# The decision of the fallback flag on VectorE, moved behind the last residual addition

## The chip, the cores and the metric

One core of one Trainium2 chip runs the whole kernel. The metric is device time in microseconds (us) of one execution; the kernel before took 322.09 us as the median of three runs (321.22, 322.09 and 322.19). The five engines are TensorE (PE; its weight loads are listed as PEld), VectorE (DVE), ScalarE (ACT), GpSimd (POOL) and SyncE (SP, which issues most DMAs). A "q" behind an engine's name, as in SPq, stands for its sequencer: instructions such as a DMA issue, a wait on a semaphore, the reading of a register or a branch, which the busy times don't count.

## What is computed

Four layers with residual additions, A, B, A, B, on x of 2048 x 512 in bfloat16, 32 heads of 16:

```python
x = A_x
x = x + _A_ref(_layernorm(x, axis=-1), A_wqkv, A_w_phi, A_wo)
x = x + _B_ref(_layernorm(x, axis=-1), B_wqkv, B_wo)
x = x + _A_ref(_layernorm(x, axis=-1), A_wqkv, A_w_phi, A_wo)
x = x + _B_ref(_layernorm(x, axis=-1), B_wqkv, B_wo)
return x
```

A is linear attention with a learned softmax feature map, B is sliding attention over 8 positions with a dilation of 2. Both end in a projection by `wo`, and its result is added to x.

## The kernel before

The program has two paths. The fast one (class `_Fast`) works on four token blocks of 512 tokens, b = 0 to 3, each held as `x[b]` with four tiles of 128 x 512, t = 0 to 3. It leaves out the subtraction of maxima in its softmaxes, which is right as long as the numbers stay small. Beside the work it gathers what tells whether they did: two sums of squares (`okc`, columns 0 and 1) and the sums of the exponentials and of their reciprocals (`stE`, `stR`). At its end it works out a flag, `fl`: 0 if all bounds hold, 1 if not. Every engine reads the flag into a register, and branches on it: with 0 it jumps over the second path (`_general_path`, a slow and safe version of the whole computation, L2063), with 1 it runs through it. With these inputs the flag is 0, so the second path isn't executed.

The flag is made by four steps in `s_flag`:

- `counts` (L1385 to L1390, DVE) compares the sums with their limits, and writes `okb`, 128 x 4.
- `total` (L1394, PE) sums `okb` over the partitions with a matmul of ones into PSUM.
- `decide` (L1398 to L1402, DVE) makes three small operations, each on the result of the one before: `ok` from the PSUM, `tot` from `ok`, `fl` from `tot`.
- `read` (L1413, all five engines) loads `fl` into a register; the branch of L2063 stands behind it.

The last layer's end is made by `s_out`. For each tile t of a block, four matmuls on PE (L542) form the projection in PSUM, one addition on DVE (L555) adds it to `x[b]`, and SP stores the result to HBM (L566). The last block to be finished, whose x is called `x_85` in the program's rows, is one of those in the table `split`: its tiles are stored one by one, 128 KB each, where other blocks store two tiles at a time, 256 KB. Each such store waits for the addition of its tile.

Behind the branch stand a few instructions on each engine: waits for its own semaphores (on SP eight of them, for the DMAs in flight; L2063 and L2090), a DRAIN, and a barrier of all five engines (L2090). The span of the profile ends with that barrier.

The order of the work is written out by hand. Each step is put on a thread by `add(stage, engine, ...)`; `run` walks through the table `_ORDER`, whose words are thread numbers in base 36, and calls the next step of that thread each time. An engine executes its instructions in just that order. The words of the flag are `iw` (DVE's thread: its first occurrence runs `counts`, its second `decide`), `ix` (`total`) and `iy` (`read`).

Of the kernel before, what the change touches and what calls it, by code (L numbers as in the profile page):

```python
# [96 lines left out]
if fh ig gb if ig gg ig gl gs ge gs fg ig gk gb gp gt gr gr gr gt ga gf ih ih if ig if ig du gr if if gs ih du  # L97
ig dv gt ii gt dw fd ig ij ij ii ik gu gu ij du gt du ij dy ik ih gu fe gs dz il gv fi gv ii ij ij im ik il fj
fk fj dx in fl iq fj ir fj dx fo iq fm is ii gw gw ij gv il ij gx ik gw il io gv gv fn fm iw gz iq ip iq iu it
gy iv it h2 gw h0 gw h2 ix iw h3 h4 h5 h3 h1 h2 h6 h3 h2 h3 h5 h7 h5 h8 h5 iy  # L100
"""


# [1991 lines left out]
```

## Time and profile before

| | us |
|---|---|
| median of three runs | 322.09 (321.22 to 322.19) |
| the profiled execution | 321.0 |
| its span, from the first to the last instruction | 319.3 |
| PE busy | 307.5 (96% of the span) |
| DVE busy | 295.6 (93%) |
| ACT busy | 274.7 (86%) |
| POOL busy | 47.3 (15%) |

The profiled execution took 321.0 us, 1.7 us more than its span: that is what lies ahead of the first and behind the last recorded instruction. Times "at 311.27" count from the start of the span. The granted TensorE clock was 0.996 of full speed. DMA share is the mean busy share of the core's 16 DMA engines, so that one engine of the 16 that works alone shows as 0.06. Issue to landing is the time from a DMA's issue on SP to the end of the last of its pieces; a store of 128 partitions is cut into 16 pieces, one for each DMA engine. The DMA queue called hardware_dynamic carries the kernel's transfers, the queues called instruction carry program code to the engines.

### The profile page before, as it was taken

To read this page: it belongs to the slowest core of one execution; us is meant where nothing else is said; L and a number is where in the kernel's file an instruction comes from. 1 tells how busy PE (TensorE), PEld (TensorE's weight loads), DVE (VectorE), ACT (ScalarE), POOL (GpSimd) and SP (SyncE) were. 2 spreads that over 40 slices of the span, in tenths; PEclk is the share of its full clock that TensorE was granted. 3 is DMA by queue.
4 is the path that set the end of the run, shared out by engine and by line. 5 is a ranking of instruction groups with operands and counts; after the bars stand their busy time and mean duration, and the time that the engine had idled before them with its cause. 6 is when DMAs were issued, how large, how long until landed. Compare 5 with 4: busy or idle time off the path is not lost. (4 is left out here: it accounts for less than half of the span.)

```text
span 319.3 us, 8889 instructions
## 1 busy us (share of the span) xinstructions
PE 307.5 (96%) x3572; PEld 152.5 (48%) x3572; DVE 295.6 (93%) x458; ACT 274.7 (86%) x638; POOL 47.3 (15%) x64
## 2 busy tenths in 40 slices
PE   8999999899999999999999999879999999999992
PEld 4644456445454444444444455534444444445550
DVE  6999995998999999999999999599997999999993
ACT  4999999999898778999999999799999777698560
POOL 6000000000004121000000000041240744035000
PEclk9999999999999999999999999999999999999998
DMA  7977100015795979949994500014389865565743
GB/s 197 351 197 154 30 2 4 2 23 146 180 156 113 153 137 137 137 83 120 158 127 54 69 0 2 4 35 117 89 171 137 149 123 127 129 163 136 172 141 132
DMA packets 45789, 36.37 MB, mean 114 GB/s; under 512 B 30832, under 2 KB 41136, under 8 KB 45744
## 3 DMA queue, kind: packets, MB, share of 16 engines
q1 hardware_dynamic: 45216, 35.75, 55.7%
q8 instruction: 29, 0.48, 0.7%
q14 instruction: 16, 0.13, 0.2%
q10 hardware_dynamic: 528, 0.02, 0.1%
HBM read 11.13 MB, written 3.25 MB: 45 GB/s over the span
## 5 line engine op out<-in xcount | busy, mean ns | idle before, releaser
L950 PE MATMUL PS<-xnT,WB 128*128 128x512 bf16 x336 | 76.8, 380 | 0.1
L1042 DVE TENSOR_TENSOR prod<-QT,K 128x4096 bf16<-128x4096 bf16 x28 | 63.4, 2287 | 0.5 <-POOL K L976 0.5
L1104 DVE TENSOR_TENSOR pav<-PT,Vg 128x4096 bf16<-128x4096 bf16 (+1 forms) x29 | 63.0, 2216 | 0.2
L950 PEld LDWEIGHTS <-WB 128*128 128x128 bf16 x336 | 37.4, 114 | 36.3 <-issue 3.3
L728 ACT ACTIVATE Eq<-PS 128x512 bf16<-128x512 f32 x64 | 36.3, 618 | 0.0
L621 ACT ACTIVATE Ek<-PS 128x512 bf16<-128x512 f32 x64 | 35.1, 623 | 0.2 <-PE PS L615 0.2
L542 PEld LDWEIGHTS <-oT 128*128 128x128 bf16 x240 | 22.3, 98 | 27.0 <-issue 1.3
L720 PE MATMUL PS<-xnT,WA 128*128 128x512 bf16 x128 | 32.0, 380 | 0.5 <-DVE s L812 0.3
L562 ACT ACTIVATE sqd<-x 128x512 bf16<-128x512 bf16 x48 | 30.0, 632 | 2.2 <-DVE x L555 2.0
L627 PE MATMUL PS<-WA,xnT 128*128 128x512 bf16 x128 | 31.6, 379 | 0.0
L555 DVE SCALAR_TENSOR_TENSOR x<-PS,x 128x512 bf16<-128x512 f32 x47 | 30.8, 685 | 0.3 <-PE PS L542 0.3
L615 PE MATMUL PS<-WA,xnT 128*128 128x512 bf16 x128 | 31.0, 379 | 0.0
L204 ACT CAST oT<-PS 128x512 bf16<-128x512 f32 (+1 forms) x50 | 26.8, 599 | 3.8 <-PE PS L1111 2.1
L542 PE MATMUL PS<-WoA,oT 128*128 128x512 bf16 x128 | 29.8, 380 | 0.0
L542 PE MATMUL PS<-WoB,oT 128*128 128x512 bf16 x112 | 27.4, 380 | 0.0
L204 ACT CAST K<-PS 128x512 bf16<-128x512 f32 x30 | 17.3, 594 | 3.1 <-PE PS L950 1.9
L615 PEld LDWEIGHTS <-xnT 128*128 128x128 bf16 x128 | 12.3, 98 | 15.1 <-issue 0.9
L627 PEld LDWEIGHTS <-xnT 128*128 128x128 bf16 x128 | 12.2, 98 | 14.5 <-issue 0.4
L673 DVE TENSOR_TENSOR Ek<-Ek,rk 128x4096 bf16<-128x4096 bf16 (+1 forms) x10 | 18.6, 1861 | 0.4 <-ACT rk L668 0.4
L465 DVE TENSOR_SCALAR xn<-x,rstd,nmr 128x512 bf16<-128x512 bf16 x48 | 18.2, 426 | 0.6
L720 PEld LDWEIGHTS <-WA 128*128 128x128 bf16 x128 | 11.6, 98 | 14.6 <-issue 1.7
L204 ACT CAST V<-PS 128x512 bf16<-128x512 f32 x26 | 15.2, 596 | 2.6 <-PE PS L950 2.6
(164 smaller groups left out, 501.6 us busy)
## 6 DMA issues: line engine op xcount, KB each, us to landing
Vg<-V SPq DMA_DIRECT2D x112, 131.5 KB, 4.3
Prho<-rd SPq DMA_DIRECT2D x8, 512.0 KB, 6.0
x<-in_A_x_dram SPq DMA_DIRECT2D x3, 512.0 KB, 6.7
WB<-in_B_wqkv_dram SPq DMA_DIRECT2D x3, 512.0 KB, 9.2
out_dram<-x SPq DMA_DIRECT2D x6, 256.0 KB, 2.2
wraw<-in_A_wqkv_dram SPq DMA_DIRECT2D x4, 256.0 KB, 4.4
vd<-Vs SPq DMA_DIRECT2D x2, 272.0 KB, 3.5
x<-in_A_x_dram SPq DMA_DIRECT2D x4, 128.0 KB, 4.6
```

What stands on the lines that cost most here:

```text
L204: self.nc.scalar.copy(out=out, in_=in_)
L542: nc.tensor.matmul(y[:], lhsT=lh(t, c), rhs=Wo()[:, c, :], start=(c == 0), stop=(c == NB - 1 and not onpe))
L555: nc.vector.scalar_tensor_tensor(out=xb[:, t, :], in0=T[t][:], scalar=1.0, in1=xb[:, t, :], op0=ALU.mult, op1=ALU.add, **kw)
L562: nc.scalar.activation(out=sqd[:], in_=xb[:, t, :], func=ACT.Square, accum_out=T["ss"][:, t:t + 1])
L615: nc.tensor.matmul(pk[:], lhsT=xnT[:, t, k, :], rhs=self.WA[:, k, D:2 * D], start=(k == 0), stop=(k == NB - 1))
L621: nc.scalar.activation(out=T["E"][:, t, s, :], in_=T["k", t][:], func=ACT.Exp, scale=1.0 - 2.0 * s)
L627: nc.tensor.matmul(pv[:], lhsT=xnT[:, t, k, :], rhs=self.WA[:, k, 2 * D:3 * D], start=(k == 0), stop=(k == NB - 1))
L720: nc.tensor.matmul(pq[:], lhsT=self.WA[:, k, hb * P:(hb + 1) * P], rhs=xnT[:, :, k, :], start=(k == 0), stop=(k == NB - 1))
L728: nc.scalar.activation(out=self.Eq[L, b][s][:, :, hb, :], in_=T[hb][:].rearrange("p (t i) -> p t i", t=4), func=ACT.Exp, scale=1.0 - 2.0 * s)
L950: nc.tensor.matmul(pp[:], lhsT=self.WB[:, k, i * D + c:(i + 1) * D:NB], rhs=xnT[:, :, k, :], start=(k == 0), stop=(k == NB - 1))
L1042: nc.vector.tensor_tensor(out=pr[:], in0=QT[:, c:c + 1, :].to_broadcast([P, NW, TB]), in1=win, op=ALU.mult)
L1104: nc.vector.tensor_tensor(out=pv, in0=PT[:, :, lo:lo + n].unsqueeze(1).to_broadcast([P, NB, 2, n]), in1=vw, op=ALU.mult)
```

## The change

One word of `_ORDER` moves: the second `iw`, which runs `decide`, goes from behind `ix` to a place behind the last additions.

```diff
-gy iv it h2 gw h0 gw h2 ix iw h3 h4 h5 h3 h1 h2 h6 h3 h2 h3 h5 h7 h5 h8 h5 iy
+gy iv it h2 gw h0 gw h2 ix h3 h4 h5 h3 h1 h2 h6 h3 h2 h3 h5 h7 h5 h8 iw h5 iy
```

On DVE the difference is this piece at the end of the fast path (names with a number are the program's buffers: `x_85` is the last block's x, `x_86` that of the block before it; `PS` is the PSUM):

```order
 L1390 TENSOR_TENSOR okb<-okc,sgn 128x4
 L555 SCALAR_TENSOR_TENSOR x_86<-PS,x_86 128x512 x2
+L555 SCALAR_TENSOR_TENSOR x_85<-PS,x_85 128x512 x4
 L1398 TENSOR_TENSOR ok<-PS,thr 128x4
 L1400 TENSOR_REDUCE tot<-ok 128x1
 L1402 TENSOR_SCALAR fl<-tot 128x1
-L555 SCALAR_TENSOR_TENSOR x_85<-PS,x_85 128x512 x4
 L1413 TENSOR_LOAD fl
 L2063 COMPARE_AND_BRANCH
```

The three operations of `decide` stood ahead of the four additions of the last block, and now stand behind them. Everything else on DVE keeps its order.

On SP, at the same place, nothing moves; these rows are the same before and after, each with the engines whose semaphores it waits for (DMAHW are those of earlier DMAs):

```order
L566 DMA out_dram<-x_85 128x512 [waits DMAHW0_49,DVE_49]
L566 DMA out_dram<-x_85 128x512 [waits DMAHW1_49,DVE_49]
L566 DMA out_dram<-x_85 128x512 [waits DMAHW2_49,DVE_49]
L566 DMA out_dram<-x_85 128x512 [waits DMAHW3_49,DVE_49]
L1413 TENSOR_LOAD fl [waits DVE_49]
L2063 COMPARE_AND_BRANCH
```

SP reads the flag behind its last store in both kernels. PE, ACT and POOL have the same rows in the same order too; each reads the flag as its last instruction ahead of the branch, and that reading waits for the moved `fl`.

## The prediction

> **What bounds the kernel now.** The page's busy table comes first, then its chain of work that ended last:
>
> ```profile
> PE 307.5 (96%) x3572; PEld 152.5 (48%) x3572; DVE 295.6 (93%) x458; ACT 274.7 (86%) x638; POOL 47.3 (15%) x64
> DVE x L555 0%
> ```
>
> PE and DVE are nearly full, but the change touches only the last 8 us. The chain ends on DVE's residual addition (L555) and says no more. The timeline of DVE and PE from 311.2 shows where that addition stands (start, duration, and so on):
>
> ```profile
> 311.27 0.16 DVE L1398 TENSOR_TENSOR ok<-PS,thr 128x4 f32<-128x4 f32 x1 [0.20 <-PE PS L1394]
> ...
> 311.66 0.15 DVE L1402 TENSOR_SCALAR fl<-tot 128x1 int32<-128x1 f32 x1
> 311.73 2.47 DVE L555 SCALAR_TENSOR_TENSOR x<-PS,x 128x512 bf16<-128x512 f32 x4
> 311.07 2.32 PE L542 MATMUL PS<-WoB,oT 128*128 128x512 bf16 x10
> ```
>
> DVE ends at 311.73 + 2.47 = 314.20, and the span at 319.3. So 5.1 us lie behind the last arithmetic, and what fills them is found on the sequencers. The reading of the flag (duration min/median/max in ns, then first and last start):
>
> ```profile
> L1413 ACTq TENSOR_LOAD <-fl x1: 714/714/714, 311.8 to 311.8; - x1
> L1413 PEldq TENSOR_LOAD <-fl x1: 737/737/737, 311.9 to 311.9; - x1
> L1413 DVEq TENSOR_LOAD <-fl x1: 711/711/711, 313.5 to 313.5; - x1
> L1413 SPq TENSOR_LOAD <-fl x1: 545/545/545, 314.6 to 314.6; - x1
> ```
>
> The branch and what stands behind it, by line:
>
> ```profile
> L2063 SPq EVENT_SEMAPHORE  x8: 17/17/17, 315.8 to 317.9; - x8
> L2063 ACTq COMPARE_BRANCH  x1: 68/68/68, 312.6 to 312.6; - x1
> L2063 PEldq COMPARE_BRANCH  x1: 482/482/482, 312.7 to 312.7; - x1
> L2063 ACTq EVENT_SEMAPHORE  x1: 17/17/17, 313.1 to 313.1; - x1
> L2063 PEldq EVENT_SEMAPHORE  x1: 51/51/51, 313.4 to 313.4; - x1
> L2063 DVEq COMPARE_BRANCH  x1: 94/94/94, 314.3 to 314.3; - x1
> L2063 SPq COMPARE_BRANCH  x1: 78/78/78, 315.3 to 315.3; - x1
> ```
>
> SP's next waits and PE's DRAIN, at the barrier's line:
>
> ```profile
> L2090 SPq EVENT_SEMAPHORE  x8: 28/28/28, 317.9 to 318.4; - x8
> L2090 PEldq DRAIN  x2: 8/8/8, 313.6 to 318.8; - x2
> ```
>
> PE was through its tail at 313.6. SP is last: its eight waits run from 315.8 to 317.9, 2.1 us, where the next eight (L2090), which find everything done, take 0.44 (a pitch of 0.065). The list of SP's waits says that it is real waiting, and the rows of the stores say for what (the last number of a row, or the triple, is us from issue to landing; the first triple is that of the last block's four stores, the next of the six earlier ones, then the first and the last of the four):
>
> ```profile
> SPq L2063 <- SPq L2063: 2.3, 4, 1.3
> 312.44 2.15 SPq L566 DMA_DIRECT2D out_dram<-x  x4
> DMA to landing us min/median/max: 1.7/2.5/3.4
> DMA to landing us min/median/max: 2.1/2.2/2.5
> out_dram<-x SPq DMA_DIRECT2D x1, 128.0 KB, 1.7
> out_dram<-x SPq DMA_DIRECT2D x1, 128.0 KB, 3.4
> ```
>
> The first of the four landed 1.7 us after its issue at 312.4, the last 3.4 us after its own (314.2), at 317.6. **The last stores' landing sets the end of the kernel.** Why 3.4 for the same 128 KB? The engines' shares by stretch (columns: stretch, its length, five engines' busy time, PE clock, DMA share, GB/s):
>
> ```profile
> 314.50:315.50 1.00, 0.00 (x0) 0.00 (x0) 0.00 (x0) 0.00 (x0) 0.00 (x0) 1.00 0.76 259
> 315.50:316.40 0.90, 0.00 (x0) 0.00 (x0) 0.00 (x0) 0.00 (x0) 0.00 (x0) 1.00 0.14 31
> 316.40:317.20 0.80, 0.00 (x0) 0.00 (x0) 0.00 (x0) 0.00 (x0) 0.00 (x0) 0.55 0.07 23
> ```
>
> By 315.5 nearly all is written. From 316.40 to 317.20 the share is 0.07, one engine of 16, working alone at a backlog. What had held it? The DMA queues in four stretches of 0.1 us, at 313.7, 314.7, 315.5 and 316.3 (packets, MB, share of 16 engines' time):
>
> ```profile
> q14 instruction: 1, 0.01, 46.2%
> ...
> q8 instruction: 1, 0.02, 67.6%
> ...
> q14 instruction: 1, 0.01, 29.9%
> ...
> q14 instruction: 1, 0.01, 35.0%
> ```
>
> These are four blocks of code on their way to the engines. The second, at 314.7, took 0.676 x 16 x 0.1 = 1.08 us on one DMA engine, until 315.8; the others 0.74, 0.48 and 0.56. Each follows a branch: 313.7 is 1.1 us behind ACT's, 314.7 is 2.0 behind PE's, 315.5 is 1.2 behind DVE's, 316.3 is 1.0 to 1.1 behind SP's. So I read the late slice as store pieces that stood behind PE's block of code, which PE's branch at 312.7 sent for. That the three early branches precede the last three stores is the point on which the forecast rests.
>
> **The change part by part.** *The additions.* The rows of one projection matmul and of the four additions (ns, first and last start):
>
> ```profile
> L542 PE MATMUL PS<-WoB,oT 128*128 128x512 bf16 x112 | 27.4, 380 | 0.0
> L555 DVE SCALAR_TENSOR_TENSOR x<-PS,x x4: 681/682/683, 311.7 to 313.5; 128x512 bf16<-128x512 f32 x4
> ```
>
> With the three operations gone, 311.73 - 311.27 = 0.46 us leave DVE ahead of the additions. The first needs its matmul, done at 311.07 + 0.38 = 311.45, so it starts at about 311.5 instead of 311.73. The last can't start before the last matmul ends, 311.07 + 2.32 = 313.39; it started at 314.20 - 0.68 = 313.52. So the last store is issued between 0 and 0.13 earlier; I take 0.03.
>
> *The flag.* From the start of `ok` to the end of `fl` it is 311.66 + 0.15 - 311.27 = 0.54 us. It now starts one pitch of the additions, (313.5 - 311.7) / 3 = 0.6 us, behind the last addition's start, at 314.1, and ends at 314.65, against 311.81: 2.8 us later. PSUM and thresholds are long there, so nothing else is waited for.
>
> *The added wait.* On ACT, POOL and PE the reading of the flag stands 2.8 us longer; behind it are only the branch, one or two waits and a DRAIN, and the barrier waits for them. PE: reading at 314.7, branch 0.8 later (311.9 to 312.7) at 315.5, DRAIN 0.9 later (312.7 to 313.6) at 316.4. SP's sixteen waits are not done before 315.8 + 16 x 0.065 = 316.8. So PE's delay is covered by 0.4 us; without that cover each further 0.1 us counts in full. DVE now waits for its own `fl`: from 313.5 to 314.7, branch 0.8 later at 315.5. Three readings at once took 714 to 737 ns and one alone (DVE) 711, so five at once cost between 0 and some tens of ns more.
>
> *SP.* Its reading started at 314.6, behind the last store's issue; `fl` is there at 314.65 to 314.7. Loss 0 to 0.1, I take 0.03. Its first wait then stands at 315.83.
>
> *The stores.* All five branches now fall between 315.3 and 315.5, and the code blocks, 1.0 to 2.0 us behind them, after 316.3. The stores' pieces of the last addition, issued at 314.2, are through by then: but for the late slice, the stretch to 315.5 held nearly all. **What the stall becomes**: between 1.7 us (the first of the four, same size) and 2.5 (the slowest of the six earlier, of twice the size). I take 1.7 to 1.8, as the nearest in size: the last store lands at 315.9 to 316.0. SP's fourth wait, which is for it, comes at 315.83 + 3 x 0.065 = 316.03. Late next is thus SP's own string of instructions. Its eighth wait starts at 315.83 + 7 x 0.065 = 316.29 instead of 317.88.
>
> *Sum:* 317.88 - 316.29 = 1.59, rounded down to 1.55 for the landing that ends almost together with the wait. With 2.5 us for the landing it is 317.6 - 316.7 = 0.9. The span becomes 317.7, the profiled execution 321.0 - 1.55 = 319.45. The median of the runs shown is 322.09, 1.1 above the profiled execution; the same 1.55 taken from it gives 320.5.
>
> **The rivals.**
> *Nothing moves.* The late slice has a cause other than the branches (one slow DMA engine, or blocks of code that come at this time anyway, as PE's queue q8 does all along). For it: code is fetched through the whole kernel. Against it: four blocks within 2.7 us, each 1 to 2 us behind a branch, and none in the 4.5 us ahead:
>
> ```profile
> q1 hardware_dynamic: 952, 0.92, 57.9%
> ```
>
> That is the only queue row from 309.2 to 313.7. Gain 0.03: 322.05.
>
> *Part of it.* A landing of 2.5 us, or a block of code that catches the last pieces: gain 0.9 or less, 321.2 to 321.8.
>
> *Code ahead of the tail.* The instructions behind the branch are not on the engine, and it stands until the block has come. Before, this would be hidden under the late landing; now it is not. PE's branch at 315.5, block 2.0 later, 1.08 long: 318.6, DRAIN 0.2 later, then the barrier, from SP's last wait at 318.4 to 319.3, 0.9: 319.7, which is 0.4 longer, 322.5. Against it: ACT's next instruction behind its branch ran at 313.1, PE's at 313.4, both ahead of the first block at 313.7. Only code a little further down could be missing.
> The Trainium skill, "Runtime: NRT & Kernel Launch", section "Instruction fetch mechanics", speaks for this rival: a taken branch to a target outside the two pages on hand makes the engine wait for a DMA of that page. By that rule the time is this rival's 322.5 rather than 320.5; the rows of ACT and PE just named don't agree with it for the first instructions, and no run here yet shows later ones.
>
> *Slower: the blocks queue up.* If that code is needed and the five blocks, now sent for within 0.2 us, go through one DMA engine with SP's last, it has its own at 316.4 + 1.08 + 0.74 + 0.48 + 0.56 = 319.3; then its unhindered string of sixteen waits and the barrier, 1.0 + 0.9: 321.2, 1.9 longer, 324.0. It decides from the point at which SP's block comes later than 317.4.
>
> **How the numbers follow.** About 0.3% (1.0 us) is what a measurement here can tell from no change. Forecast 0.62, and only it is faster by more than that. Nothing moves 0.16, part of it 0.10, code ahead of the tail 0.06: together 0.32 within 0.3%. Queueing 0.06, slower. The time is the forecast's, 320.5. The range takes in the scatter of the runs (321.22 to 322.19, so 0.6 below the forecast) and reaches up over part of it and nothing moves: 319.9 to 322.2. Left out above are the two code rivals, 0.12.
>
> **What would show it.** In the profile after: the last store lands within 2 us; `fl` ends near 314.65, and all readings start there; SP's eight waits take some 0.5 us instead of 2.1; no stretch with a DMA share of one engine before 316.2; the code blocks come after 316.3. A landing that stays above 3 us with the blocks behind it proves me wrong on the cause; waits of SP that are done early and a span that stays shows the code rivals.

## The result, and the profile after

The changed kernel took 320.24 us (median of 5 runs, 319.88 to 320.68), the kernel before 321.49 beside it (5 runs). The ratio is 0.996, with a 95% interval of 0.9948 to 0.9973: 0.9 to 1.7 us faster. The forecast was 320.5, 1.55 us faster. In the second batch of runs below, one execution of the kernel before took 1102.21 us; it is left out of that batch's comparison, and what happened in it isn't on record.

The profiled execution took 320.68 us with a span of 318.9. Read it from the end, as before. DVE's timeline:

```profile
312.52 2.70 DVE L555 SCALAR_TENSOR_TENSOR x<-PS,x 128x512 bf16<-128x512 f32 x4 [0.40 <-PE PS L542]
315.14 0.15 DVE L1398 TENSOR_TENSOR ok<-PS,thr 128x4 f32<-128x4 f32 x1
315.33 0.16 DVE L1400 TENSOR_REDUCE tot<-ok 128x1 f32<-128x4 f32 x1
315.52 0.15 DVE L1402 TENSOR_SCALAR fl<-tot 128x1 int32<-128x1 f32 x1
```

The last addition ends at 312.52 + 2.70 = 315.22, a whole microsecond later than the 314.20 of before. That isn't the change: a second profile of the kernel before (`before_look`, below) has that end at 315.3. What lies upstream shifts by about 1 us from execution to execution. So the two kernels are compared here by the **tail**, from the end of the last addition to the end of the span: 319.3 - 314.2 = 5.1 us before, 318.9 - 315.2 = 3.7 after. The 1.3 to 1.4 us between them are the measured gain (321.49 - 320.24 = 1.25).

The place that the three operations left, 0.46 us, is now mostly a wait of DVE for PE (0.40 in the first row): it gained nothing for the additions. From the start of `okb` (L1390) to the end of the last addition it is 314.20 - 309.72 = 4.48 us before and 315.22 - 310.76 = 4.46 after.

The branches, SP's string of waits, and the stores (issues on SP, then issue to landing, min/median/max of the four):

```profile
L2063 SPq EVENT_SEMAPHORE  x8: 17/17/17, 317.0 to 317.6; - x8
L2063 ACTq COMPARE_BRANCH  x1: 68/68/68, 316.5 to 316.5; - x1
L2063 SPq COMPARE_BRANCH  x1: 78/78/78, 316.5 to 316.5; - x1
L2063 PEldq COMPARE_BRANCH  x1: 487/487/487, 316.6 to 316.6; - x1
L2063 PEldq EVENT_SEMAPHORE  x1: 51/51/51, 317.1 to 317.1; - x1
```

```profile
L566 SPq DMA_DIRECT2D out_dram<-x x4: 332/341/350, 313.2 to 315.3; - x4
DMA to landing us min/median/max: 1.7/1.7/1.7
```

SP's eight waits take 0.6 us where they took 2.1, and all four stores land in 1.7 us; the last one took 3.4. The engines' shares by stretch show the same without any semaphore:

```profile
316.00:316.60 0.60, 0.00 (x0) 0.00 (x0) 0.00 (x0) 0.00 (x0) 0.00 (x0) 1.00 0.62 219
316.60:317.40 0.80, 0.00 (x0) 0.00 (x0) 0.00 (x0) 0.00 (x0) 0.00 (x0) 1.00 0.00 0
317.40:318.90 1.50, 0.00 (x0) 0.00 (x0) 0.00 (x0) 0.00 (x0) 0.00 (x0) 0.53 0.10 27
```

The stretch in which one engine of 16 worked off a backlog (share 0.07) is gone; after 316.6 nothing is written. What moves behind it is code. The queues from 310.3 to 317.5 (first row: the kernel's transfers are the only ones), and from 317.5 to 317.8:

```profile
q1 hardware_dynamic: 1392, 1.31, 51.9%
...
q14 instruction: 3, 0.02, 31.4%
q8 instruction: 1, 0.02, 20.6%
```

Four blocks of code, all that move in these rows, now start about 1 us behind the five branches, when the stores are done.

### The profile page after: what moved, and what is told of

Read it like the earlier page. It is cut to its first block, busy times and chain, and to the rows that moved or that the text cites. A ratio compares the mean times of both kernels' runs of the same rounds, so it can differ in the third digit from the quotient of the medians.

```text
span 318.9 us, 8889 instructions
## 1 busy us (share of the span) xinstructions
PE 307.8 (97%) x3572; PEld 153.0 (48%) x3572; DVE 296.0 (93%) x458; ACT 274.7 (86%) x638; POOL 47.3 (15%) x64
## 4 chain that ended last, share of the span: by engine, by line
PE 87%; ACT 7%; DVE 2%; POOL 1%; issue 1%; DVEq 0%; ACTq 0%
PE PS L950 22%; PE PS L542 17%; PE PS L615 9%; PE PS L627 9%; PE PS L720 6%; PE PS L1111 4%; PE PS L1049 4%; PE PS L1168 2%; ACT Eq L728 2%; PE PS L690 2%; PE PS L308 2%; POOL vh L992 1%; PE PS L923 1%; PE PS L481 1%; PE PS L545 1%; PE PS L1183 1%
```

## The experiments

Theory 1 is the prediction's: the block of 16 KB that PE's branch sends for holds one DMA engine, and with it the pieces of the last stores. The rivals: it is the blocks of ACT and POOL that do it (A); the gain comes from the place that DVE's operations leave ahead of the additions (B); a later flag is simply better, however it is made (C). The sizes are those of the queues' rows for the whole execution before: q8 moved 29 blocks with 0.48 MB, 16 KB each, and q14 16 blocks with 0.13 MB, 8 KB each. That q8 is PE's queue is read from its moving with PE's branch in every kernel below. Each ratio is against the kernel before in the same batch.

### Which engine's branch: pe_late and actpool_late

In both the decision stays where it was before. A second copy of its last operation is made behind the last addition, and some engines read the copy:

```diff
+        def late():
+            self.fl2 = self.sm([1], "fl2", I32, 1)
+            nc.vector.tensor_scalar(out=self.fl2[:], in0=T["tot"][:], scalar1=4.0, scalar2=None, op0=ALU.not_equal)
...
+        regs = nc.alloc_registers("redo", engines=mybir.ALL_ENGINES)
+        for reg in regs:
+            src = self.fl2 if reg.engine in LATE else self.fl
+            nc.engines[reg.engine].reg_load(reg, src[0:1, 0:1])
```

`LATE` is PE alone in the first, ACT and POOL in the second. Expected of PE alone:

> Only PE reads a late flag: the flag is decided early as before, a copy of its last operation stands behind the last addition, and PE alone waits for that copy. ACT and POOL branch early, as before. The tail, from the end of the last addition to the end of the span, is 5.1 us before the change and 3.7 after it. Theory 1 (the 16 KB block of code that PE's branch sends for holds store pieces): the last store lands in 1.7 to 1.9 us, the tail is 3.4 to 3.7, and the time falls by 1.2 to 1.7 us. Rival A (the 8 KB blocks of ACT and POOL hold them): landing stays near 3.4 us, tail near 5.1, no gain. Rival B (the gain comes from the 0.46 us of DVE that leave the place ahead of the four additions): those three operations are still there, so no gain.

Expected of ACT and POOL:

> The mirror of the run before: ACT and POOL wait for the late copy of the flag, PE reads the early one. Theory 1: PE's block of code comes at the same point as before the change, so the last store lands in 3.2 to 3.5 us, the tail is 4.9 to 5.2, and there is no gain (within 0.3 us). Rival A: landing 1.7 to 1.9, tail 3.4 to 3.7, gain 1.2 to 1.7 us. Rival B: no gain.

Measured: pe_late 0.9964 (0.9951 to 0.9978), 320.54 us against 321.61; actpool_late 1.001 (0.9998 to 1.0023). The gain of pe_late, 1.1 us, is a little under the expected 1.2 to 1.7, its tail of 3.6 is as expected. pe_late's branches of ACT and PE, the landing of its last four stores, and its blocks of code in short stretches at 314.4 (the one sent for by the early branches) and 316.8:

```profile
L2063 ACTq COMPARE_BRANCH  x1: 68/68/68, 313.3 to 313.3; - x1
L2063 PEldq COMPARE_BRANCH  x1: 490/490/490, 315.6 to 315.6; - x1
...
DMA to landing us min/median/max: 1.7/1.7/1.8
...
q14 instruction: 1, 0.01, 36.7%
...
q8 instruction: 1, 0.02, 119.9%
```

The same of actpool_late, with the issues of its stores, and its block of PE in the stretch from 315.0 to 315.1:

```profile
L2063 PEldq COMPARE_BRANCH  x1: 486/486/486, 313.8 to 313.8; - x1
L2063 ACTq COMPARE_BRANCH  x1: 68/68/68, 315.9 to 315.9; - x1
...
L566 SPq DMA_DIRECT2D out_dram<-x x4: 333/351/1901, 313.4 to 315.2; - x4
DMA to landing us min/median/max: 1.7/3.5/3.9
...
q8 instruction: 1, 0.02, 105.3%
```

With PE alone late, the block q8 starts at 316.8 and the stores land in 1.7 to 1.8 us, although ACT's and POOL's early branches still send for an 8 KB block in the middle of them. With PE early and ACT and POOL late, q8 starts at 315.0, takes 1.053 x 16 x 0.1 = 1.7 us, and the stores land late. The row of the issues shows a second way of being late: SP's issue of the last store took 1.90 us, and what stands behind it on SP waited (more on this at `before_look`). **PE's block is the one, rival A falls, and B with it**, since the three operations stand ahead of the additions in both.

### Only the last operation late: fl_late, fl_late_again

```diff
-        def decide(): ok, tot, fl
+        def decide(): ok, tot
+        def last(): fl
-gy iv it h2 gw h0 gw h2 ix iw h3 h4 h5 h3 h1 h2 h6 h3 h2 h3 h5 h7 h5 h8 h5 iy
+gy iv it h2 gw h0 gw h2 ix iw h3 h4 h5 h3 h1 h2 h6 h3 h2 h3 h5 h7 h5 h8 iw h5 iy
```

(The first three lines are shortened; `last` is the third step on DVE's thread of the flag.)

> Only the last of the three operations of the decision moves behind the last addition, two stay ahead of the four additions, and all engines read the late flag. Theory 1: landing 1.7 us, and since the flag is there 0.38 us earlier than in the changed kernel, SP's string starts right behind the last store's issue: tail 3.4 to 3.6, a gain of 1.4 to 1.7 us over before, 0.1 to 0.3 better than the changed kernel. Rival B: only a third of the 0.46 us leaves DVE's place ahead of the additions, so a third of the gain, 0.4 us.

Measured: 0.9957 (0.9942 to 0.9973), 320.16 us. The second time it ran in one batch with the changed kernel:

> The kernel in which only the last of the three operations of the decision is late, on the same chip as the changed kernel. Its first profile had a tail of 3.5 us against 3.7. If SP's later reading of the flag is what the changed kernel loses against the forecast, it is 0.1 to 0.3 us faster than the changed kernel, which is at the edge of what 5 rounds tell apart; SP's first wait again at 1.56 us behind the end of the last addition. If the loss is elsewhere, the two are equal in tail.

> The changed kernel once more, beside the others of this batch: 1.0 to 1.5 us faster than before, tail 3.7 us (from the end of the last addition to the end of the span), the last store lands in 1.7 us, SP's first wait behind the branch 1.8 us behind the end of the last addition. If the first comparison was luck, the interval takes in 1.

Measured: fl_late_again 0.9948 (0.9931 to 0.9966), 320.02 us; the changed kernel 0.996 (0.9944 to 0.9975), 320.3. The intervals overlap; by time the two aren't told apart. Their tails are, in two profiles each: 3.5 and 3.5 against 3.7 and 3.7. The rows of fl_late_again (additions, SP's reading, SP's waits; its span is 318.5):

```profile
312.33 2.64 DVE L555 SCALAR_TENSOR_TENSOR x<-PS,x 128x512 bf16<-128x512 f32 x4
...
L1414 SPq TENSOR_LOAD <-fl x1: 546/546/546, 315.4 to 315.4; - x1
...
L2063 SPq EVENT_SEMAPHORE  x8: 17/17/17, 316.5 to 317.1; - x8
```

And of after_again, with a span of 318.6:

```profile
312.17 2.71 DVE L555 SCALAR_TENSOR_TENSOR x<-PS,x 128x512 bf16<-128x512 f32 x4 [0.39 <-PE PS L542]
...
L1413 SPq TENSOR_LOAD <-fl x1: 720/720/720, 315.3 to 315.3; - x1
...
L2063 SPq EVENT_SEMAPHORE  x8: 17/17/17, 316.7 to 317.2; - x8
```

SP's reading takes 546 ns in the one and 720 in the other, and its first wait comes 1.5 to 1.6 us behind the last addition's end (315.0) against 1.8 (314.9). That is where the changed kernel falls short of what a late flag can give. Rival B gave this kernel a third of the gain; it has all of it.

### The places between: mid2 and mid3

One word again: the second `iw` stands behind `h6` (after the second of the last four additions) or behind `h7` (after the third).

> The decision stands in the middle, behind the second of the last four additions. Theory 1 gives an order that isn't monotone: PE's branch comes at 314.1 instead of 312.7, its block of code holds a DMA engine from some 315.1 to 317.2, and the piece of the last store (data from 315.3) falls into it: landing 3.4 to 4.0 us, tail 4.8 to 5.6, and the time is 0.3 to 0.9 us longer than before, though the flag is later. Rival B and any rival by which a later flag is simply better: about half of the gain, 0.6 us faster than before, landing in between.

> The decision stands behind the third of the last four additions. In the runs so far the block of code starts 1.3 to 2.0 us behind PE's branch. Here PE's branch comes some 0.3 us behind the end of the last addition, so nothing holds an engine before 1.3 us behind that end, and the last store's data are written by 1.35 us. Theory 1: landing 1.7 to 2.2 us, tail 3.4 to 3.9, so 1.0 to 1.6 us faster than before, where the place one addition earlier was 0.3 us slower than before. If the gain grew evenly with the delay of the flag, it would lie between the place behind the second addition (0.3 us slower) and the changed kernel (1.3 us faster): 0.5 us faster. One additional cost: the last addition starts 0.25 us later.

Measured: mid2 1.0015 (1.0004 to 1.0026), slower than before by 0.1 to 0.8 us; mid3 0.9959 (0.9945 to 0.9973), 1.3 us faster. mid2, with its PE branch, the block in the stretch from 315.85 to 315.95, the longest landing, SP's waits, and the DMA engines' share behind the last issue (315.0):

```profile
L2063 PEldq COMPARE_BRANCH  x1: 488/488/488, 314.6 to 314.6; - x1
...
q8 instruction: 1, 0.02, 98.5%
...
DMA to landing us min/median/max: 1.7/1.7/3.6
...
SPq L2063 <- SPq L2063: 2.4, 2, 1.9
...
316.60:317.40 0.80, 0.00 (x0) 0.00 (x0) 0.00 (x0) 0.00 (x0) 0.00 (x0) 1.00 0.08 20
317.40:318.20 0.80, 0.00 (x0) 0.00 (x0) 0.00 (x0) 0.00 (x0) 0.00 (x0) 1.00 0.06 10
```

The block takes 0.985 x 16 x 0.1 = 1.6 us, until about 317.5. From 317.4 to 318.2 a single engine of 16 still writes (0.06), so what is left of the last store stands behind the block and follows it.

mid3, with the block in the stretch from 316.40 to 316.45:

```profile
L2063 PEldq COMPARE_BRANCH  x1: 482/482/482, 315.2 to 315.2; - x1
...
q8 instruction: 1, 0.02, 185.8%
...
DMA to landing us min/median/max: 1.7/1.7/1.7
```

The gain doesn't grow with the delay of the flag (rival C). At mid2 three stores escape the block and the last one's piece on that DMA engine stands behind it, at mid3 all four escape: PE's branch is 0.6 us later, and 0.5 us of loss (by the ratio) become 1.3 us of gain. In both, the three operations between the additions cost 0.2 us of their own: from the start of `okb` to the end of the last addition it is 4.7 us instead of 4.5. That is why mid2 loses 0.5 us though its tail is only 0.2 longer than before.

### Without flag and branch: no_flag; the kernel before once more: before_look

no_flag leaves out the reading, the branch and the whole second path, and with them the hint of the branch at the program's start:

```diff
-        add("flag", "ALL", read)
...
-    with tc.If(redo > 0, label="redo"):
-        _general_path(tc, A_x, A_wqkv, A_w_phi, A_wo, B_x, B_wqkv, B_wo, out)
```

> Leaves out the reading of the flag, the branch and the whole second path; the decision itself is still worked out, at its early place. No engine branches, so no block of code is sent for behind the last stores. Theory 1: landing 1.7 us, and only the landing and SP's string behind it are left: tail 3.3 to 3.45 us, 1.5 to 1.9 us faster than before, so the late flag has recovered nearly all that the flag costs at the end. Rival (a slow DMA engine that has nothing to do with the branches): landing stays above 2.5 us, tail above 4.

Measured: 0.9924 (0.9911 to 0.9936), 319.32 us, 2.5 us faster than before. From 311 to its end at 318.3 no block of code moves. Its transfers, SP's two waits, and its string at L2090:

```profile
q1 hardware_dynamic: 1392, 1.31, 51.2%
...
SPq L2090 <- DMA out_dram<-x: 1.3, 1, 1.3
SPq L2090 <- PEq L2090: 0.6, 2, 0.4
...
L2090 SPq EVENT_SEMAPHORE  x7: 17/28/28, 317.3 to 318.3; - x7
```

SP goes from its last issue straight to waiting for the stores (1.3 us), and then to the barrier (0.6). The landing is as expected. The tail of 2.8 us is shorter than the expected 3.3 to 3.45, and the gain of 2.5 us larger than the expected 1.5 to 1.9: with the branch gone SP also has fewer waits, seven in all (the last two at the barrier) where the kernel before has eighteen (eight at L2063, ten at L2090). The expectation that the late flag recovers nearly all of the flag's cost fails with it. So the late flag recovers the 1.3 us of the stores, and the flag still costs about 1 us (320.3 against 319.3). Reading, branch and string are what no_flag lacks on SP; how the 1 us divides among them was not measured.

> The kernel before, unchanged, for a second profile. Theory 1: as in the first, the last store lands 3.2 to 3.5 us after its issue, PE's block of code starts 1.3 to 2.1 us behind PE's branch, and the tail is 4.9 to 5.2 us. If the late landing were an accident of one execution, landing is near 1.7 us and the tail near 3.5.

Measured (one execution, 322.13 us): tail 320.4 - 315.3 = 5.1, the landing late again, PE's branch at 313.9 and its block in the stretch from 315.0 to 315.1, 1.1 us behind it, a little sooner than expected:

```profile
312.82 2.47 DVE L555 SCALAR_TENSOR_TENSOR x<-PS,x 128x512 bf16<-128x512 f32 x4
...
L566 SPq DMA_DIRECT2D out_dram<-x x4: 332/351/1940, 313.5 to 315.3; - x4
DMA to landing us min/median/max: 1.7/3.5/3.9
...
L2063 PEldq COMPARE_BRANCH  x1: 393/393/393, 313.9 to 313.9; - x1
q8 instruction: 1, 0.02, 117.4%
...
L1413 SPq TENSOR_LOAD <-fl x1: 551/551/551, 317.3 to 317.3; - x1
L2063 SPq EVENT_SEMAPHORE  x8: 17/17/17, 318.5 to 319.0; - x8
```

The tail is that of the first profile, but the time goes elsewhere. There SP issued the last store in 0.36 us, and its eight waits took 2.1 us for the landing. Here the block was on its way, until 315.0 + 1.174 x 16 x 0.1 = 316.9, when SP came to the last store. The issue took 1.94 us, until 317.2. The reading of the flag started behind it at 317.3, and the eight waits, late as a whole, took only 0.5 us. So the block delays the end in two ways: through the pieces that stand behind it, or, when SP issues during it, through the issue. actpool_late is of the second kind (issue 1.90 us, waits 318.4 to 319.0), mid2 of the first.

All kernels side by side (us; block: start of q8 behind PE's branch; the tail counts from the end of the last addition):

| kernel | PE's branch, against the end of the last addition | block behind the branch | slowest landing of the four | tail | ratio |
|---|---|---|---|---|---|
| before | -1.5 | 2.0 | 3.4 | 5.1 | 1 |
| before_look | -1.4 | 1.1 | 3.9 | 5.1 | |
| actpool_late | -1.4 | 1.2 | 3.9 | 5.2 | 1.001 |
| mid2 | -0.4 | 1.3 | 3.6 | 5.3 | 1.0015 |
| mid3 | 0.3 | 1.2 | 1.7 | 3.5 | 0.9959 |
| fl_late | 0.8 | 1.1 | 1.7 | 3.5 | 0.9957 |
| pe_late | 0.8 | 1.2 | 1.8 | 3.6 | 0.9964 |
| after | 1.3 | 1.2 | 1.7 | 3.7 | 0.996 |
| no_flag | none | none | 1.7 (the last four) | 2.8 | 0.9924 |

The 2.0 us between branch and block in the first profile didn't recur; all later ones are 1.1 to 1.3. What made it longer is open.

## Why the prediction was right, step by step

**The cause** was the step on which the forecast rested, and it holds: the pair pe_late and actpool_late separates PE's block from those of ACT and POOL, mid2 and mid3 show the edge. The rival that nothing moves falls. One part of the path is narrower than the forecast had it: "The last stores' landing sets the end of the kernel" is true of the profile that it read, while in before_look the same block took its time at SP's issue of the last store. A branch behind the stores removes both.

**The level.** 320.5 against the measured 320.24 looks closer than the forecast of the gain was. The gain was put 0.3 us too high (1.55 against 1.25), and the start 0.6 too high (322.09, the median of the first three runs, against 321.49 of five). That the two errors partly offset each other is luck.

**The additions.** Predicted: hardly anything for them, 0.03 us. Measured: 4.48 - 4.46 = 0.02. DVE's freed place became a wait for PE of 0.40 us.

**The flag** was to end 0.45 us behind the last addition (314.65 against 314.20); it ends 315.52 + 0.15 - 315.22 = 0.45 behind it.

**The stores** were to land in 1.7 to 1.8 us: 1.7.

**SP's string** is where the size is off. Predicted tail gain 1.55, measured 5.1 - 3.7, that is 1.3 to 1.4. The mis-sized step is that five readings at once cost "between 0 and some tens of ns more". It was taken from 711 to 737 ns on the other engines (with POOL's 758, which stands in the same view, the three at once took 714 to 758), while the sum gave SP's reading the 545 ns that it took before. SP's took 713 in the first profile and 720 in the second, 0.17 us more:

```profile
L1413 SPq TENSOR_LOAD <-fl x1: 713/713/713, 315.7 to 315.7; - x1
```

And it took the string's pitch, 0.065 us, from eight waits at L2090; the first eight at L2063 took 0.5 to 0.6 us for seven steps (317.0 to 317.6 here, 316.7 to 317.2 in after_again), where seven steps of 0.065 are 0.46: about 0.1 more. Together that is 0.2 to 0.3 us, the missing part. fl_late, in which the reading is 545 ns again, has 0.2 us less tail.

**Code ahead of the tail** and the slower rival that grew out of it didn't come: PE's next instruction ran at 317.1, SP's at 317.0, and the first block moves after 317.5. The Trainium skill, "Runtime: NRT & Kernel Launch", section "Instruction fetch mechanics", has an engine wait for the page behind a taken branch if the page isn't on hand; here, with all five branches at the end of the path, no engine waited for one. Each engine is given a hint of the branch at the program's start (L2090, BRANCH_PREFETCH_HINT, at 0.8 to 0.9 us). Whether that is why was not tried, and whether the target's page was on hand the traces don't show.

**PE's cover**: its tail was to end 0.4 us ahead of SP's. PE's DRAIN ran at 317.2 (L2090), SP's string of sixteen ends at 318.1, so the cover held, with 0.9.

The chances put faster by over 0.3% at 0.62; the ratio of 0.996 lies there, the interval reaches down to 0.27%.

## What to carry to other kernels

When the chain of work ends microseconds ahead of the span, read the tail from the sequencers and the DMA queues: what lands last, and what else used the DMA engines then. Here a taken branch cost more than its own time, because it sent for code over the engines that carried the last stores, and a branch placed so that its block fell behind the last bytes was worth 1.3 us, more than a flag that is ready early. Try such a place at several positions, since an edge of 0.6 us decided here between slower and faster, and compare tails rather than whole spans where the upstream shifts by 1 us, with what the change costs ahead of the tail added (0.2 us in mid2).

## What the runs showed of the hardware beside that

- A block of code reaches back to the engine that issues. Where PE's block came in the middle of the four stores (actpool_late, before_look), the issue of the last store took SP 1.90 and 1.94 us instead of 0.33 to 0.36, and ended 0.3 to 0.4 us behind the block. SP's reading of the flag then started only at 317.2 and 317.3. The same stands in the kernel before far ahead of the branches: an earlier store's issue at 302.0 took 1.77 us, until 303.8, and a block on q8 was on its way from about 301.9 to 303.4. That full queues on the held DMA engine are the reason is an inference; no run tested it. Long issues occur without such a block too (2.0 us at 12.8, among the loads at the start).
- The same reading of one register took 545 to 556 ns on SP in most kernels, 713 and 720 in the two runs of the changed one, and on the other engines from 467 to 797. What decides between them wasn't looked for.
- A block of 8 KB for ACT or POOL in the middle of the stores (pe_late) cost the landing at most 0.1 us, the 16 KB of PE 1.7 to 2.2 (before, before_look, actpool_late, mid2).
